# A decode kernel with two attention parts: a shorter unrolled head ahead of VectorE's loop, and a third buffer for output weights

## The chip, the cores and the metric

The kernel runs on one core of one Trainium2 chip. The metric is the device time of one execution in microseconds, lower is better. Executions of one kernel differ by some us (the kernel before: 1383.4 to 1388.7 in its first six), so each comparison below uses several executions of both kernels on one chip. The span on a profile page is some 2.1 us shorter than the time of the same execution.

## The reference

Two independent decode attentions on one token, four batches, head size 128, 512 model columns; their outputs are joined side by side.

```python
def _A_ref(x, k_cache, v_cache, wq, wo):      # "sliding" part: 32 query heads, 8 KV heads
    W = min(4096, max(256, Sk // 4))          # Sk = 8192, so W = 2048: only the last 2048 positions
    q = (x @ wq).reshape(B, Sq, Hq, Dh) ...
    k = jnp.repeat(k_cache[:, :, Sk - W:, :], rep, axis=1)      # v likewise, rep = 4
    p = softmax(einsum("bhqd,bhkd->bhqk", q, k) * Dh ** -0.5)
    return einsum("bhqk,bhkd->bhqd", p, v) ... @ wo

def _B_ref(x, k_cache, v_cache, wq, wo):      # "full" part: 32 heads, the whole cache of 8192
    ...                                       # the same without the window and the repeat
return jnp.concatenate([a, b], axis=-1)
```

Nearly all bytes are the caches: 2 x 268 MB for the full part, 2 x 16.8 MB for the sliding part.

## The kernel before

Work is cut into 72 chunks: 0 to 7 are the sliding part (2 MB of keys and 2 MB of values each), 8 to 71 the full part (4 MB and 4 MB). For every chunk TensorE transposes the key tiles into PSUM (`tr`), VectorE and ScalarE copy them to SBUF (`kt`), TensorE multiplies them with the queries (`sc`), and the softmax and the product with the values (`po`) follow one chunk later. SyncE issues all loads in a fixed order; each waits until its place in `kv`, ten halves of 2 MB, is free.

```python
NWO = 2                                    # buffers of the sliding part's output weights
...
HALF_A = {"k": (8, 9), "v": (6, 7)}        # halves of kv for sliding keys and values
...
def dma_wo(g):                             # output weights of sliding chunk g
    dst = wor[:, g % NWO, :] ...
    sch.add_dma("sp", lambda e: e.dma_start(dst, src), "d_wo%d" % (g % NWO),
                waits=[("fin", g - NWO)] if g >= NWO else [], key=("wo", g))
...
def dma_kv(kind, c):
    at = HALF_A[kind][c % 2] if ch["ab"] == 0 else (0 if kind == "k" else 4) + 2 * (c % 2)
    waits = take((kind, c), at, 1 if ch["ab"] == 0 else 2, ("T", ch["s_last"]) if kind == "k" else ("pv", c))
    ...
    sch.add_dma("sp", lambda e: e.dma_start(dst, src), "d_h%d" % at, waits=waits, key=(kind, c))
```

So full keys use halves 0 to 3, full values 4 to 7, and keys of chunk c wait for the last transpose of chunk c - 2.

Each engine's program is first recorded straight, with a mark before every second chunk. Stretches between marks that are the same but for fixed steps then become one loop; everything ahead of them stays unrolled.

```python
def emit_looped(self, engname, eng, sems, loop):
    for first, n, a, step in self.runs(engname):       # equal stretches between marks
        self.emit_ops(ops[done:m[first]], eng, sems)   # unrolled part
        with loop(0, n) as i:
            self.emit_ops(ops[m[a]:m[a + 1]], eng, sems, step, i, a - first)
...
sch.emit_looped("dve", e, sems, loop_on(mybir.EngineType.DVE, 0))   # slot 0: aligned loop head
```

At the first full chunk there is no chunk before it, so a dummy chunk (`NONE`) stands in. Its VectorE work differs from the later ones, so VectorE's stretch of chunks 8 and 9 doesn't match and stays unrolled:

```python
def norm_sum(c):
    if c == NONE:
        pe_mm(ms[:, L0:L0 + 4], onesf[:, :], rst[1][:, :], waits=ms_read, key=("L", c))
        sch.add("dve", lambda e: e.memset(rz[:, :], 0.0), waits=[("L", c)], key=("rinv", c))
        sch.add("dve", lambda e: e.memset(oz[:, :], 0.0), key=("rz", c))
        ...
        return
    ...
def norm_out(c):
    if c == NONE:
        sch.add("dve", lambda e: e.memset(oz[:, :], 0.0), waits=[("pv", c), ("rz", c)], key=("oT", c))
        ...
```

## Time and profile before

| what | value | read from |
|---|---|---|
| median, 3 runs | 1384.63 us (1383.43 to 1386.19) | times |
| profiled execution | 1388.1 us (span 1386.0) | times and page |
| bytes, mean rate | 587.56 MB, 424 GB/s | page, slices |
| steady rate, 200 to 1340 us | 431 GB/s | stretches |
| packets of the instruction queue q14 | 8 of 8 KiB | page, queues; sizes from the trace |

In the lines of profiles below, `[6.16 <-issue]` says that the engine stood idle for 6.16 us just before, and that the profile shows nothing that it waited for; `<-PE tr` names what it waited for. A load lands when its bytes are there; its 16 transfer engines finish one by one, so it has a first and a last landing (values 10 in before: 183.43 and 186.70 us). A hole is a stretch in which the load queue runs dry.

### The profile page before, as it was taken

The page shows a single profiled execution, that of the slowest core. Times are in us where ns is not written, and L with a number is a line of the kernel's source. Part 1 is how long each engine was busy: PE and PEld are TensorE (multiplying, and loading weights), DVE is VectorE, ACT ScalarE, POOL GpSimd, SP SyncE. Part 2 cuts the span into 40 slices and gives each one's busy share as a digit, 9 for nine tenths or more (in the row PEclk, how much of TensorE's full clock was granted, in tenths as well). Part 3 has the DMA queues.
Part 4 walks back from the last instruction along what each step waited for, and adds up shares of the span by engine and source line. Part 5 has one row for each costly group of instructions (what it writes and reads, how often), then busy time and mean ns, then how long its engine had stood idle before and what let it go on. Part 6 is the DMA issues. An engine that isn't in the chain of part 4 may idle for free.

```text
span 1386.0 us, 59254 instructions
## 1 busy us (share of the span) xinstructions
PE 1181.4 (85%) x26901; PEld 1137.5 (82%) x26901; DVE 640.3 (46%) x1337; ACT 436.2 (31%) x649; POOL 4.5 (0%) x16
## 2 busy tenths in 40 slices
PE   4888789888888888888898889888988889888988
PEld 4776789887888888887888888887988888787987
DVE  1665355444444444444444445444444445444443
ACT  1553233332333223332333223232332233232332
POOL 1000000000000000000000000000000000000000
PEclk9998999999999999999999999999999999999998
DMA  9999989999999999999999999999999999999997
GB/s 400 414 416 410 424 351 429 431 436 429 428 431 434 427 432 433 428 432 430 431 427 436 430 427 436 430 428 429 436 430 427 436 430 427 430 436 429 428 431 320
DMA packets 30088, 587.56 MB, mean 424 GB/s; under 512 B 2784, under 2 KB 10992, under 8 KB 11248
## 3 DMA queue, kind: packets, MB, share of 16 engines
q1 hardware_dynamic: 30040, 587.22, 99.1%
q8 instruction: 16, 0.26, 0.1%
q14 instruction: 8, 0.07, 0.0%
q10 hardware_dynamic: 24, 0.01, 0.0%
HBM read 587.21 MB, written 0.01 MB: 424 GB/s over the span
## 4 chain that ended last, share of the span: by engine, by line
DMA 59%; PE 37%; DVE 2%; issue 1%; ACT 0%; SPq 0%; ACTq 0%; DVEq 0%
DMA kv<-in_B_k_cache_dram 57%; PE tr L367 21%; PE sc L369 10%; PE po L369 3%; PE fin L369 2%; DMA kv<-in_B_wq_dram 2%; DVE sA L482 1%; PE ms L369 1%; DVE kt L431 0%; DVE rm L491 0%; DVE sA L480 0%; ACT pba L545 0%; PE ms L367 0%; DVE outsb L640 0%; ACT kt L429 0%
## 5 line engine op out<-in xcount | busy, mean ns | idle before, releaser
L367 PE MATMUL tr<-identb,kv 128*128 128x128 bf16 x8704 | 705.5, 232 | 156.6 <-DMA kv<-in_B_k_cache_dram 154.3
L431 DVE COPY kt<-tr 128x1024 bf16<-128x1024 bf16 x736 | 502.6, 691 | 478.2 <-PE tr L367 471.6
L367 PEld LDWEIGHTS tr<-identb,kv 128*128 128x128 bf16 x8704 | 560.9, 105 | 182.1 <-issue 97.6
L429 ACT ACTIVATE kt<-tr 128x1024 bf16<-128x1024 bf16 x352 | 360.2, 1024 | 635.5 <-PE tr L367 634.9
L369 PE MATMUL sc<-qb,kt 128*128 128x64 bf16 x8704 | 449.6, 197 | 15.7 <-DVE kt L431 15.4
L369 PEld LDWEIGHTS sc<-qb,kt 128*128 128x128 bf16 x8704 | 371.5, 101 | 19.8 <-DVE kt L431 17.2
L369 PE MATMUL po<-pbb,kv 128*128 128x64 bf16 (+1 forms) x8320 | 293.9, 191 | 6.6 <-issue 6.6
L369 PEld LDWEIGHTS po<-pbb,kv 128*128 128x128 bf16 x8320 | 267.0, 97 | 8.6 <-issue 6.9
L530 ACT ACTIVATE pbb<-sc,negb 64x128 bf16<-64x128 f32 x128 | 51.2, 400 | 295.9 <-DVE negb L520 295.2
L496 DVE TENSOR_REDUCE rm<-sc 64x1 f32<-64x128 f32 x128 | 37.0, 289 | 92.5 <-PE sc L369 91.6
L508 DVE TENSOR_REDUCE gm<-ms 1x2 f32<-1x128 f32 (+1 forms) x72 | 20.1, 279 | 44.5 <-PE ms L367 44.4
L520 DVE COPY negb<-ms 128x1 f32<-128x1 f32 (+1 forms) x72 | 11.4, 159 | 57.4 <-PE ms L369 57.4
L369 PE MATMUL ms<-identf,gx 1*128 1x1 f32 (+1 forms) x144 | 27.7, 259 | 0.0
L369 PEld LDWEIGHTS ms<-identf,gx 1*128 1x128 f32 (+1 forms) x144 | 21.5, 187 | 4.9 <-issue 0.9
L530 ACT ACTIVATION_READ_ACCUMULATOR pbb<-sc,negb 64x1 f32 x128 | 23.7, 185 | 0.0
L367 PE MATMUL ms<-identf,rm 128*1 128x128 f32 (+1 forms) x72 | 19.6, 273 | 2.3 <-DVE rm L491 2.3
L369 PE MATMUL po<-pba,kv 128*128 128x64 bf16 x512 | 20.1, 199 | 0.5 <-ACT pba L545 0.5
L369 PE MATMUL fin<-wos,oz 128*4 128x512 bf16 x66 | 20.0, 385 | 0.3 <-DVE oz L620 0.3
L369 PEld LDWEIGHTS po<-pba,kv 128*128 128x128 bf16 x512 | 17.9, 102 | 0.6 <-ACT pba L545 0.6
L512 DVE TENSOR_SCALAR gx<-gm 1x128 f32<-1x128 f32 (+1 forms) x72 | 15.9, 221 | 2.5
L369 PE MATMUL ms<-xT,kv 128*128 128x4 bf16 x256 | 7.1, 166 | 8.6 <-DMA kv<-in_A_wq_dram 4.4
L369 PEld LDWEIGHTS ms<-xT,kv 128*128 128x128 bf16 x256 | 7.0, 104 | 8.8 <-DMA kv<-in_A_wq_dram 4.5
(49 smaller groups left out, 138.3 us busy)
## 6 DMA issues: line engine op xcount, KB each, us to landing
kv<-in_B_k_cache_dram SPq DMA_DIRECT2D x64, 4096.0 KB, 26.5
kv<-in_B_v_cache_dram SPq DMA_DIRECT2D x63, 4096.0 KB, 31.4
kv<-in_A_k_cache_dram SPq DMA_DIRECT2D x8, 2048.0 KB, 13.7
kv<-in_A_v_cache_dram SPq DMA_DIRECT2D x8, 2048.0 KB, 15.8
kv<-in_A_wq_dram SPq DMA_DIRECT2D x1, 4096.0 KB, 12.4
kv<-in_B_wq_dram SPq DMA_DIRECT2D x1, 4096.0 KB, 27.5
wor<-in_A_wo_dram SPq DMA_DIRECT2D x8, 512.0 KB, 10.7
wos<-in_B_wo_dram SPq DMA_DIRECT2D x16, 256.0 KB, 22.0
```

Of the source, the lines that this page charges most:

```text
L367: sch.add("pe", lambda e: e.transpose(o, l, r), waits, key)
L369: sch.add("pe", lambda e: e.matmul(o, l, r, start=start, stop=stop), waits, key)
L429: sch.add("act", lambda e: e.activation(dst, src, ACTF.Copy), waits=waits, key=("ev", s))
L431: sch.add("dve", lambda e: e.tensor_copy(dst, src), waits=waits, key=("ev", s))
L482: emit = lambda e, src=src, b=b: e.scalar_tensor_tensor(out=t, in0=src, scalar=mk[:, b:b + 1], in1=t, op0=ALU.mult, op1=ALU.add)
L496: sch.add("dve", lambda e, src=src, pp=pp: e.tensor_reduce(out=rm[pp, m, 0:1], in_=src, axis=AX.X, op=ALU.max), waits=[("S", ch["s_last"]) ...
L508: sch.add("dve", lambda e: e.tensor_reduce(out=gm[0:C, m, 0:U], in_=src, axis=AX.X, op=ALU.max), waits=[("trm", c)], key=("gmax", c))
L512: sch.add("dve", lambda e: e.tensor_scalar(out=dst, in0=gv, scalar1=-scale, scalar2=None, op0=ALU.mult), waits=[("gmax", c)], key=("gx", c))
L520: sch.add("dve", lambda e: e.tensor_copy(negb[:, m, 0:C], ms[:, col:col + C]), waits=[("bc", c)], key=("negb", c))
L530: sch.add("act", lambda e, src=src, pp=pp, n=n, u=u: e.activation(pbv[pp, :, u], src, ACTF.Exp, bias=negb[pp, m, 0:1], scale=scale, accum_ ...
```

## The change

Intent: "VectorE and ScalarE enter their loops with the tensor engine, the absent chunk masked by zeros; last sliding-block output weights have a buffer of their own". The dummy chunk gets the same VectorE instructions as every later chunk: its reciprocal runs on ones, its mask is a block of zeros in front of `pm`. So VectorE's stretch of chunks 8 and 9 matches and joins the loop. The weights of sliding chunk 7 get a third buffer, which moves the sliding values and one weight load to other halves of `kv`.

```diff
-NWO = 2
+NWO = 3
...
-        pm = sb("pm", [P, HB // 2, 2, 2, 4], F32)
+        pm = sb("pm", [P, HB // 2 + 1, 2, 2, 4], F32)
...
+            sch.add("pool", lambda e, own=own: e.memset(own, 1.0), ...)      # cut: ones for the dummy sums
...
-        HALF_A = {"k": (8, 9), "v": (6, 7)}
+        HALF_A = {"k": (8, 9), "v": (4, 5)}
...
+        def wo_slot(g):
+            return g % 2 if g < NCA - 1 else 2
...
-            sch.add_dma("sp", lambda e: e.dma_start(dst, src), "d_wo%d" % (g % NWO),
-                        waits=[("fin", g - NWO)] if g >= NWO else [], key=("wo", g))
+            sch.add_dma("sp", lambda e: e.dma_start(dst, src), "d_wo%d" % slot,
+                        waits=[("fin", g - 2)] if g >= 2 and slot < 2 else [], key=("wo", g))
...
-        dma_wq(1, 2)
+        dma_wq(1, 6)
...
         def norm_sum(c):
-            if c == NONE:
-                ... three memsets and a return, as shown above
+            if c >= NCA or c == NONE:
+                pair = 4 * (c - NCA - 1 + 4) if c != NONE else 8             # masks start with zeros
...
         def norm_out(c):
-            if c == NONE:
-                sch.add("dve", lambda e: e.memset(oz[:, :], 0.0), ...)
```

More of the change, by code (lines that the diff above doesn't have):

```diff
@@ L262, in bass_concat_heads__sliding_block_cached__mha_block_cached__decode_kernel @@
             fill=0.0, base=0, channel_multiplier=-1), waits=["c_onesf"], key="c_identf")
-        sch.add("pool", lambda e: e.memset(rst[1][:, :], 0.0), key="c_rs")
-        sch.add("pool", lambda e: e.memset(qb[:, :, :], 0.0), key="c_qb")
+        sch.add("pool", lambda e: e.memset(rst[1][:, :], 0.0), key="c_rs0")
+        for u in range(2):
+            own = rst[1][u * P // 2:(u + 1) * P // 2, :].rearrange("p (b u) -> p u b", u=2)[:, u, :]
+            sch.add("pool", lambda e, own=own: e.memset(own, 1.0), waits=["c_rs0"], key="c_rs" if u else None)
+        sch.add("pool", lambda e: e.memset(qb[:, :, :], 0.0), waits=["c_rs"], key="c_qb")
         sch.add("pool", lambda e: e.memset(pm[:, :, :, :, :], 0.0), key="c_pm0")
         for x in range(2):
-            sch.add("pool", lambda e, x=x: e.memset(pm[:, :, x, x, :], 1.0), waits=["c_pm0"], key="c_pm" if x else None)
+            sch.add("pool", lambda e, x=x: e.memset(pm[:, 1:, x, x, :], 1.0), waits=["c_pm0"], key="c_pm" if x else None)
         sch.add("pool", lambda e: e.memset(pbt[0][:, :, :], 0.0), key=("c_pb", 0))
@@ L295, in dma_wq @@
             sch.add_dma("sp", lambda e: e.dma_start(flat(at, 2), src), "d_h%d" % at, waits=waits, key=("wq", ab))
+        def wo_slot(g):
+            return g % 2 if g < NCA - 1 else 2
         def dma_wo(g):
             src = A_wo[g * 4 * P:(g + 1) * 4 * P, :].rearrange("(hl d) n -> d hl n", d=P)
-            dst = wor[:, g % NWO, :].rearrange("p (hl n) -> p hl n", hl=4)
-            sch.add_dma("sp", lambda e: e.dma_start(dst, src), "d_wo%d" % (g % NWO),
-                        waits=[("fin", g - NWO)] if g >= NWO else [], key=("wo", g))
+            slot = wo_slot(g)
+            dst = wor[:, slot, :].rearrange("p (hl n) -> p hl n", hl=4)
+            sch.add_dma("sp", lambda e: e.dma_start(dst, src), "d_wo%d" % slot,
+                        waits=[("fin", g - 2)] if g >= 2 and slot < 2 else [], key=("wo", g))
         def dma_wos(hp):
@@ L583, in norm_sum @@
         def norm_sum(c):
-            if c == NONE:
-                pe_mm(ms[:, L0:L0 + 4], onesf[:, :], rst[1][:, :], waits=ms_read, key=("L", c))
-                sch.add("dve", lambda e: e.memset(rz[:, :], 0.0), waits=[("L", c)], key=("rinv", c))
-                sch.add("dve", lambda e: e.memset(oz[:, :], 0.0), key=("rz", c))
-                ms_read[:] = [("rinv", c)]
-                rs_read[NSM] = [("L", c)]
-                return
-            if chunks[c]["ab"] == 0:
+            if 0 <= c < NCA:
                 m, n, rs, ri = c % NSM, 16, rst[0][:, c % NSM, :], rinv[:, c % NSM, :]
@@ L594, in norm_sum @@
                 m, n, rs, ri = NSM, 4, rst[1][:, :], rinv[:, 0, 0:4]
-            pe_mm(ms[:, L0:L0 + n], onesf[:, :], rs, waits=[("rs", c), "c_onesf"] + ms_read, key=("L", c))
+            pe_mm(ms[:, L0:L0 + n], onesf[:, :], rs, waits=([("rs", c), "c_onesf"] if c != NONE else []) + ms_read, key=("L", c))
             sch.add("dve", lambda e: e.reciprocal(out=ri, in_=ms[:, L0:L0 + n]), waits=[("L", c)], key=("rinv", c))
-            if chunks[c]["ab"] == 1:
-                pair = 4 * (c - NCA - 1)
+            if c >= NCA or c == NONE:
+                pair = 4 * (c - NCA - 1 + 4) if c != NONE else 8
                 pv = pm[:, :, :, :, :].rearrange("p a b c d -> p (a b c d)")
@@ L607, in norm_out @@
         def norm_out(c):
-            if c == NONE:
-                sch.add("dve", lambda e: e.memset(oz[:, :], 0.0), waits=[("pv", c), ("rz", c)], key=("oT", c))
-                po_read[:] = [("oT", c)]
-                return
-            if chunks[c]["ab"] == 0:
+            if 0 <= c < NCA:
                 m = c % NSM
@@ L618, in norm_out @@
                 i1 = rz[:, :].rearrange("p (x y) -> p x y", x=2)
-            waits = [("rinv" if c < NCA else "rz", c), ("pv", c)] + ([("fin", c - 2 if c != NCA + 1 else NONE)] if c >= 2 else [])
+            waits = [("rinv" if 0 <= c < NCA else "rz", c), ("pv", c)] + ([("fin", c - 2 if c != NCA + 1 else NONE)] if c >= 2 else [])
             sch.add("dve", lambda e: e.tensor_tensor(out=o, in0=i0, in1=i1, op=ALU.mult), waits=waits, key=("oT", c))
@@ L630, in emit_fin @@
             else:
-                w = wor[:, c % NWO, :].rearrange("p (hl n) -> p hl n", hl=4)
+                w = wor[:, wo_slot(c), :].rearrange("p (hl n) -> p hl n", hl=4)
                 ov = oT[:, c % NSM, :].rearrange("p (u c) -> p u c", c=REP)
```

## The prediction

> **What bounds the kernel now.** The page comes first. It says that bytes bound this kernel: 587 MB pass, the transfer engines are in use in nearly every slice, and the chain that ended last is mostly the load of the full cache's keys.
>
> ```profile
> DMA  9999989999999999999999999999999999999997
> GB/s 400 414 416 410 424 351 429 431 436 429 428 431 434 427 432 433 428 432 430 431 427 436 430 427 436 430 428 429 436 430 427 436 430 427 430 436 429 428 431 320
> ...
> DMA 59%; PE 37%; DVE 2%; issue 1%; ACT 0%; SPq 0%; ACTq 0%; DVEq 0%
> ```
>
> The reader is to see the rate of about 430 that holds from slice 7 to 39, and one hole in it: slice 6, 173 to 208 us, with 351. As the bytes stay the same, only the holes can be won. A table by stretch sizes them (columns: stretch, length, busy time of each engine, granted clock, DMA share, GB/s).
>
> ```profile
> 103.00:113.00 10.00, 8.30 (x120) 6.44 (x117) 6.61 (x18) 5.19 (x8) 0.00 (x0) 0.83 0.91 359
> ...
> 130.00:183.00 53.00, 41.51 (x861) 40.06 (x859) 20.70 (x42) 14.11 (x20) 0.00 (x0) 0.87 1.00 425
> 183.00:190.00 7.00, 7.00 (x178) 7.00 (x177) 4.48 (x9) 3.07 (x3) 0.00 (x0) 1.00 0.19 70
> 190.00:200.00 10.00, 10.00 (x258) 9.86 (x255) 5.57 (x13) 3.49 (x7) 0.00 (x0) 1.00 0.99 406
> 200.00:1340.00 1140.00, 988.62 (x22818) 961.51 (x22816) 530.96 (x1084) 353.15 (x529) 0.00 (x0) 0.94 1.00 431
> ```
>
> Against its neighbours' 425 GB/s, the hole at 183 us cost 7 x (1 - 70/425) = 5.8 us, the refill after it 10 x (1 - 406/431) = 0.6 us, and a small hole at 103 to 113 us 10 x (1 - 359/425) = 1.6 us. Together 8.0 us of 1385, that is 0.6%. From 200 to 1340 us nothing is to be had.
>
> Why the queue ran dry is read from the issues on SyncE's queue. Chunks 0 to 7 are the sliding part, 8 to 71 the full part; a full chunk has a key and a value load of 4 MB, at 4.19 MB / 430 GB/s = 9.75 us each.
>
> ```profile
> 103.25 0.54 SPq L322 DMA_DIRECT2D kv<-in_A_v_cache_dram  x1
> 111.05 0.37 SPq L300 DMA_DIRECT2D wor<-in_A_wo_dram  x1
> ...
> 161.41 0.33 SPq L334 DMA_DIRECT2D kv<-in_B_k_cache_dram  x1
> 170.40 0.33 SPq L334 DMA_DIRECT2D kv<-in_B_v_cache_dram  x1
> 189.00 0.33 SPq L334 DMA_DIRECT2D kv<-in_B_k_cache_dram  x1
> ```
>
> The load of 170.40 (values 10) has landed on the first engine at 183.4 us, on the last at 186.7 (the trace's semaphore events). The next, keys 12, waits until TensorE has transposed chunk 10 and goes out at 189.00. TensorE was late because VectorE stood still:
>
> ```profile
> 169.94 0.16 DVE L443 COPY qb<-qs 128x2 bf16<-128x2 bf16 x1
> 176.26 1.29 DVE L431 COPY kt<-tr 128x1024 bf16<-128x1024 bf16 x2 [6.16 <-issue]
> ```
>
> ```profile
> 168.52 0.80 PE L369 MATMUL po<-pbb,kv 128*128 128x64 bf16 x22 [3.45 <-issue]
> ...
> 177.01 0.61 PE L369 MATMUL sc<-qb,kt 128*128 128x64 bf16 x8 [4.16 <-DVE kt L431]
> ```
>
> The 6.16 us sit between the branch into VectorE's loop and its first instruction, with no semaphore to wait for. [...] ScalarE enters its loop too, at 130 us, and there branch and first instruction are 0.5 us apart.
>
> [...] a packet of the instruction queue starts at 174.2 us, inside the 6.16 us. [...] the packets of VectorE's and ScalarE's queue are of 8192 bytes (TensorE's of 16384)[...]. [...] the trace shows 0.50 from 176.5 to 182.6 us, behind the 4.16 us stop.
>
> **The change part by part.**
>
> 1. VectorE's loop. The built programs differ by 37 VectorE instructions: chunks 8 and 9 leave the unrolled part (192 instructions become 155) and the loop runs 31 times in place of 30. ScalarE's program is the same, in spite of the description: it runs 32 times already. Where does the branch land? Single instruction packets start at 58.0 and 152.7 us, when VectorE has done 50 and 178 recorded instructions. The difference is 128[...]. So the 6.16 us should not move to 129 us but vanish, down to ScalarE's 0.5 us.
>
> What that gives: chunk 10's keys part starts at 170.18 us in both. The next chunk, undisturbed, needs 204.85 - 193.78 = 11.1 us for it. The fetch stall of TensorE's own first pass (3.45 us at 165 to 168.5) stays, and with it the half clock of 169.6 to 172.7 us, worth some 1.3 us. Keys 12 are issued at 170.2 + 11.1 + 1.3 = 182.6, in place of 189.00.
>
> 2. The buffer for the last output weights. Now the weights of 111.05 us wait for a free buffer, and behind them the full part's first loads. With a third buffer they go out at about 104 us. At that time 7.7 us of work is pending (values 7 lands first at 111.0), and weights and keys 8 and 9 add 9.2 MB = 21.3 us, so the queue lasts to 132.3 us and the hole of 1.6 us closes. In the trace values 8 landed first at 144.4; they would land at 142.1, 2.3 us earlier.
>
> 3. Moved halves of the buffer. Sliding values now sit where values 8 go, so that load waits for the last sliding product, 127.4 us, in place of going out at 113.0. The queue lasts to 132, so nothing is lost. Values 9 wait for the absent chunk's product at 148 us as before.
>
> 4. Masks. Two memsets of 64x2 on GpSimd, done near 5 us, in a stretch where it has nothing else of use, and a reciprocal and two products (0.18 + 0.17 + 0.17 us by the later rows) for three memsets of 0.06 on VectorE, which has 0.67 us gaps there. Zero.
>
> The sum, by first landings: values 8 at 142.1, keys 10 at 151.8, values 9 at 161.6. Keys 11 are issued at 161.4 as before, since TensorE's first pass (128.87 to 170.18 us for what later takes 31) is held by its own fetches. A new load needs 0.95 us to its first packet (189.00 to 189.95), so 0.8 us are lost; keys 11 land at 172.1, values 10 at 181.9. Keys 12, issued at 182.6, start at 183.6: 1.7 us lost. They land at 193.3, against 200.7 before: 7.4 us. But the last engine counts. It lagged by 3.3 us ahead of the hole and by 0.5 us after it, as the hole let it catch up; the two short gaps let it catch up by only 2.5, so 0.8 remain: last landing 194.1 against 201.16, 7 us at best. Restarts and uneven engines will take some of it; I put the gain at 5.5 us. From there all is bound by bytes, and the gain is carried to the end: 1384.6 - 5.5 = 1379.1 us.
>
> **The rivals.**
> (a) The stall moves with the branch: [...] VectorE fetches at 130 us. Then keys 8 end some 5 us late, keys 10 go out at 145 while the queue is dry at 142, and everything TensorE does until 180 us shifts. Against it: ScalarE's entry at the same time took 0.5 us[...]. It would leave 1 to 3 us of gain: 1382 to 1384.
> (b) TensorE's own fetches are what bounds 128 to 183 us, so that the early gain of part 2 is taken back at keys 11 and 12. For it: four stops "issue" of 0.7 to 3.5 us in that pass. It is partly in my sum; in full it leaves about 4 us: 1380.5.
> (c) The stall is fully hidden by the byte bound. Against it: the 70 GB/s. It would give 1384.6.
> (d) Both holes close without new ones: 8.0 us, 1376.6.
>
> **Range and chances.** The runs before spread over 1383.4 to 1386.2, so a median is good to about 1 us. Low is (d) less that, 1376.0; high is (a), 1383.0. 2% would be 27.7 us, over three times all holes together, so faster gets 0.01; slower by as much would need a new wait in every round of a loop whose instructions are the same, 0.01.
>
> **What would show it.** The idle "issue" row of VectorE's copies into kt gone (6.2 us to under 1); keys 12 issued near 182.6 us; the output weights issued behind values 7 at 104; a stretch 183 to 190 us at over 330 GB/s and 103 to 113 at 420; 431 GB/s from 200 to 1340 as before. I am wrong if VectorE stops for 6 us at 130, or if keys 12 come at 187 or later, or if a new hole over 3 us opens between 140 and 185.

Cut from the recorded text, at the marks, is what it told of the hardware that no trace or run of this case shows; the expectations below have cuts of the same kind. With it goes the reason why the stop was to vanish rather than move: a count of where VectorE's branch and its loop head lie. No term of the sum is cut. The sum assumes that the stop is gone, and comes to keys 12 issued at 170.2 + 11.1 + 1.3 = 182.6 us and landed last at 194.1 in place of 201.16, 7 us at best, put at 5.5: 1384.6 - 5.5 = 1379.1 us. The 0.50 is the granted TensorE clock.

## More of the kernel before

From the profile page of the kernel before: the busy times of the engines, then two rows of the DMA queues (packets, MB, share of 16 engines' span).

```profile
PE 1181.4 (85%) x26901; PEld 1137.5 (82%) x26901; DVE 640.3 (46%) x1337; ACT 436.2 (31%) x649; POOL 4.5 (0%) x16
...
q1 hardware_dynamic: 30040, 587.22, 99.1%
...
q14 instruction: 8, 0.07, 0.0%
```

The reader is to see that the load queue takes 99.1% of all engines' time while TensorE is at 85%: this kernel is bound by bytes, and less than 1% of the span has transfer engines without a load.

## The result, and the profile after

| | before | after |
|---|---|---|
| median of 6 runs | 1385.76 us (1383.43 to 1388.65) | 1381.39 us (1380.30 to 1381.74) |
| ratio, 95% interval | | 0.9967 (0.9954 to 0.9980) |
| span of the profiled execution | 1386.0 | 1379.5 |

Ratios are the mean time of one kernel's runs over that of the other's of the same rounds, so not quite the ratio of the medians quoted. The gain is 4.4 us by medians and 4.6 by the ratio (0.0033 x 1385.8), 0.3%. The two spans differ by 6.5 us, but the profiled execution of before was a slow one, 1388.1 us, 2.4 above the median of six.

The page of the kernel after: span, slices, chain and instruction queue.

```profile
span 1379.5 us, 59295 instructions
...
GB/s 401 414 417 424 427 410 431 431 430 430 431 429 435 427 433 430 430 432 429 434 427 434 431 429 431 430 432 429 434 429 431 431 430 432 429 434 429 431 431 319
...
q14 instruction: 6, 0.05, 0.0%
```

Slice 6 rose from 351 to 410 GB/s, all slices after it stand where they stood, and two instruction packets are gone. The stretches of the kernel after (columns as in the prediction; the last three are granted TensorE clock, DMA share and GB/s):

```profile
103.00:113.00 10.00, 8.29 (x168) 7.11 (x166) 6.65 (x18) 6.10 (x9) 0.00 (x0) 1.00 1.03 408
130.00:183.00 53.00, 44.66 (x992) 43.39 (x990) 23.27 (x46) 15.92 (x22) 0.00 (x0) 0.90 1.00 423
183.00:190.00 7.00, 7.00 (x183) 6.86 (x180) 4.19 (x11) 2.06 (x6) 0.00 (x0) 1.00 0.96 360
190.00:200.00 10.00, 10.00 (x256) 9.51 (x253) 5.38 (x9) 3.96 (x4) 0.00 (x0) 1.00 1.01 436
200.00:1340.00 1140.00, 984.52 (x22690) 957.24 (x22687) 529.34 (x1081) 351.32 (x527) 0.00 (x0) 0.93 1.00 431
```

The hole at 183 us went from 70 to 360 GB/s and the small one at 103 from 359 to 408; the steady 1140 us are untouched. VectorE around its loop entry in the kernel after:

```profile
126.03 0.68 DVE L638 CAST outsb<-fin 4x512 bf16<-4x512 f32 x1 [1.26 <-PE fin L377]
126.77 1.29 DVE L439 COPY kt<-tr 128x1024 bf16<-128x1024 bf16 x2
```

The first copy inside the loop follows the last unrolled instruction by 126.77 - 126.71 = 0.06 us. Before, the first loop copy came 6.16 us late. The stop did not move, it is gone. SyncE's issues after:

```profile
103.62 0.60 SPq L308 DMA_DIRECT2D wor<-in_A_wo_dram  x1
...
104.81 0.94 SPq L342 DMA_DIRECT2D kv<-in_B_k_cache_dram  x2
124.52 0.33 SPq L342 DMA_DIRECT2D kv<-in_B_v_cache_dram  x1
...
159.72 0.33 SPq L342 DMA_DIRECT2D kv<-in_B_k_cache_dram  x1
...
181.44 0.33 SPq L342 DMA_DIRECT2D kv<-in_B_k_cache_dram  x1
```

The output weights go out at 103.62 us where they waited until 111.05, and keys 12 at 181.44 in place of 189.00.

### The profile page after: what moved, and what is told of

It reads as the page before. It is cut to its first block, busy times and chain, and to the rows that moved or that the text cites. A ratio compares the mean times of both kernels' runs of the same rounds, so it can differ in the third digit from the quotient of the medians.

```text
span 1379.5 us, 59295 instructions
## 1 busy us (share of the span) xinstructions
PE 1175.3 (85%) x26901; PEld 1132.3 (82%) x26901; DVE 640.6 (46%) x1337; ACT 435.7 (32%) x649; POOL 4.8 (0%) x18
## 4 chain that ended last, share of the span: by engine, by line
DMA 59%; PE 37%; DVE 2%; issue 1%; ACT 0%; SPq 0%; ACTq 0%; DVEq 0%
DMA kv<-in_B_k_cache_dram 57%; PE tr L375 22%; PE sc L377 10%; PE po L377 3%; DMA kv<-in_B_wq_dram 2%; PE fin L377 2%; DVE sA L490 1%; PE ms L377 1%; DVE kt L439 0%; DVE rm L499 0%; DVE sA L488 0%; ACT pba L553 0%; PE ms L375 0%; ACT kt L437 0%; DVE sA L546 0%
## 5 line engine op out<-in xcount | busy, mean ns | idle before, releaser
L377 PE MATMUL sc<-qb,kt 128*128 128x64 bf16 x8704 | 448.0, 196 | 11.1 <-DVE kt L439 10.7
```

The costliest lines, as they stand in the source:

```text
L377: sch.add("pe", lambda e: e.matmul(o, l, r, start=start, stop=stop), waits, key)
```

## The experiments

Twelve runs were made, in four batches, each batch sharing its runs of the kernel before. Where a trace is quoted it is of one execution. The interval of a ratio is about 0.2% wide to each side, 2.6 us, so differences below that are not resolved by a single comparison.

| run | edit | median us | ratio to before (95%) |
|---|---|---|---|
| after_again | the change itself | 1381.34 | 0.9969 (0.9951 to 0.9988) |
| loop_only | change without its buffer part | 1381.12 | 0.9972 (0.9954 to 0.9991) |
| buffer_only | before with the buffer part | 1384.49 | 1.0002 (0.9981 to 1.0023) |
| head_free | before, loop head of VectorE not aligned | 1382.12 | 0.9973 (0.9955 to 0.9992) |
| head_free_buffer | the same and the buffer part | 1381.20 | 0.9968 (0.9948 to 0.9987) |
| pad_16 | change, 16 more VectorE instructions | 1380.80 | 0.9964 (0.9944 to 0.9983) |
| pad_32 | change, 32 more | 1381.35 | 0.9965 (0.9947 to 0.9984) |
| pad_48 | change, 48 more | 1385.71 | 1.0002 (0.9982 to 1.0021) |
| split_keys | change, all full key loads halved | 1383.67 | 0.9984 (0.9965 to 1.0003) |
| split_last | change, last key load alone halved | 1378.52 | 0.9960 (0.9940 to 0.9979) |
| split_two | change, key loads 12 and 71 halved | 1380.22 | 0.9964 (0.9946 to 0.9982) |
| split_last_again | split_last once more | 1378.55 | 0.9958 (0.9940 to 0.9977) |

The theory to be tested, as far as runs can decide it: VectorE's stop of 6.16 us, inside which a packet of the instruction queue starts (174.18 us), belongs to the entry branch into the aligned loop and depends on how many instructions stand ahead of it; the stop delayed chunk 10's transposes, so keys 12 were issued late and the load queue ran dry. The change cuts the unrolled part from 192 to 155 instructions, and with that the stop. Rivals: the gain comes from the buffer; or it comes from the masked instructions themselves; or from the early loop entry as such, however many instructions stand ahead of it.

### The change again, and its two parts one by one

> The changed kernel once more, as the yardstick for the runs beside it. Every theory expects a ratio to the kernel before near the first one, 0.9967 (0.995 to 0.998), VectorE's idle 'issue' ahead of its copies into kt under 1 us, and keys 12 issued near 181.5 us.

It repeated: 0.9969, keys 12 issued at 178.29 us. (The issue time moves by some us between executions; see the end of this part.)

```diff
  loop_only, against the kernel after:
-NWO = 3
+NWO = 2
-        HALF_A = {"k": (8, 9), "v": (4, 5)}
+        HALF_A = {"k": (8, 9), "v": (6, 7)}
-            return g % 2 if g < NCA - 1 else 2
+            return g % 2
-        dma_wq(1, 6)
+        dma_wq(1, 2)
```

> The masks and VectorE's earlier loop alone; two weight buffers and the old places of the halves, as in the kernel before. My theory: VectorE's 6.2 us stop is gone, keys 12 come near 182 us, and as the queue with the small hole left at 103 to 113 us holds work until 183.4, no hole opens at 183. So this part alone gives the whole gain: ratio 0.9967, within 0.0008 of the changed kernel. Rival, the parts add up: the hole of 1.6 us at 103 to 113 stays as a loss, ratio near 0.998.

The stretch at the hole in loop_only:

```profile
183.00:190.00 7.00, 7.00 (x156) 6.51 (x154) 4.11 (x6) 3.26 (x4) 0.00 (x0) 1.00 1.01 435
```

435 GB/s: no hole at all, keys 12 issued at 176.28 (182 was expected), no stop on VectorE, and 0.9972: the loop part alone gives as much as the whole change, within the intervals.

```diff
  buffer_only, against the kernel before (the mirror of it):
-NWO = 2
+NWO = 3
-        HALF_A = {"k": (8, 9), "v": (6, 7)}
+        HALF_A = {"k": (8, 9), "v": (4, 5)}
+        def wo_slot(g):
+            return g % 2 if g < NCA - 1 else 2
...                                            # cut: dma_wo and its reader take wo_slot, as in the change
-        dma_wq(1, 2)
+        dma_wq(1, 6)
```

> The third weight buffer and the moved halves alone; VectorE enters its loop at chunk 10 as before. My theory: the output weights go out at 104 us and the hole at 103 to 113 closes, but keys 12 still come near 188 to 189 us behind the 6.2 us stop, so that the hole at 181 to 190 grows by the same 1.6 to 2.3 us: ratio 0.999 to 1.000. Rival, the parts add up: ratio near 0.9988.

First the hole's stretch, then VectorE's first copy in the loop, both of buffer_only:

```profile
183.00:190.00 7.00, 7.00 (x206) 6.94 (x202) 3.14 (x7) 1.93 (x2) 0.00 (x0) 1.00 0.62 225
```

```profile
173.08 1.29 DVE L434 COPY kt<-tr 128x1024 bf16<-128x1024 bf16 x2 [5.33 <-issue]
```

The weights and the first full keys went out early as intended (keys 8 at 104.03 us), yet the stop of 5.33 us is still there, keys 12 come at 185.60, and the hole with them. They were expected at 188 to 189; this execution began chunk 8 at 125.2 us, 3.6 earlier than the traced one of before, and all behind it is earlier by as much. Ratio 1.0002; up to 2.6 us of gain would be inside its interval, but none shows. So the two parts don't add: each of them alone or together works on the same budget, the bytes that can be delivered by the time keys 12 are issued. Bytes brought in earlier only make the queue run dry earlier, as long as the issue of keys 12 stands.

One caution for reading the traces of this stretch: chunk 8 started its keys part at 125.9 us in the profiled execution of after and at 127.6 in after_again, the same kernel; at 128.9 in before and 130 in head_free and pad_32. Such shifts move all issue times behind them. So the times above were judged with the durations of stops, which don't depend on it.

### Is it the entry into the aligned loop?

```diff
  head_free, against the kernel before:
-            sch.emit_looped("dve", e, sems, loop_on(mybir.EngineType.DVE, 0))
+            sch.emit_looped("dve", e, sems, loop_on(mybir.EngineType.DVE))
```

The work and its order stay. VectorE's loop head is no longer aligned, and with that the branch that enters the loop goes: the trace has 30 branches of this loop in place of 31, the first only at 201.48 us, behind the first round.

> The kernel before, with one word changed: VectorE's loop head is not aligned[...]. Chunks 8 and 9 stay unrolled, no masks, two weight buffers. [...] the stop at 170 us is gone (under 1 us), keys 12 near 182 to 183 us, ratio 0.996 to 0.9975, as with the masks. Rival, the stop belongs to entering the loop two chunks late, or to any entry into a loop: the stop stays at about 6 us and the ratio at 1.000.

VectorE's first loop copy in head_free:

```profile
170.75 1.29 DVE L431 COPY kt<-tr 128x1024 bf16<-128x1024 bf16 x2 [0.55 <-PE tr L367]
```

The 6.16 us that ended with "issue" are 0.55 us that end with TensorE's product, keys 12 go out at 180.76, and the ratio is 0.9973. This one option gives as much as the whole change, within the intervals, with no mask, no longer loop and no third buffer. This rules out that the masked instructions or the early entry as such are needed. It shows that the stop hangs on the entry branch, but not on what else: the branch itself is gone. For that there are the kernels that keep it, after and loop_only above and the three that follow.

> The kernel before with the third weight buffer and moved halves and the unaligned loop head on VectorE, no masks. My theory: the same as the changed kernel, ratio 0.9965 within 0.0008, keys 12 near 181.5 us. Rival, the masks matter in themselves: slower than the changed kernel by over 0.1%.

With the buffer part on top (the two diffs above together) the ratio was 0.9968, keys 12 at 179.84. As expected, the change's gain is had without its main edit.

The other direction is to bring the stop back with the change in place, by idle instructions on VectorE ahead of the loop:

```diff
  pad_16, pad_32, pad_48 (N = 16, 32, 48), against the kernel after:
+        pads = sb("pads", [P, N], F32)
...
+        for i in range(N):
+            sch.add("dve", lambda e, i=i: e.memset(pads[:, i:i + 1], 0.0))
```

They run at the very start, where VectorE has little else to do (busy 0.55 of the first 10 us in before).

> The changed kernel with 16 memsets of one column on VectorE at its very start, where it waits for data anyway. [...] no stop near 127 us (under 1 us), ratio as the changed kernel (0.996 to 0.998). [...]

> As the run with 16, but 32 memsets: [...] My theory: VectorE stops for 4 to 7 us at its loop entry near 127 us with no semaphore to wait for, TensorE waits behind it, keys 10 are issued 3 to 6 us later than with 16, and the ratio is 0.998 to 1.000 (gain of 0 to 3 us left). Rival[...]: no stop and the same time as with 16, within 0.1%.

> The changed kernel with 48 memsets in front of VectorE's program. The run with 32 did not stop at its loop entry, [...] the block ahead of the loop has 155 + 32 = 187 instructions there and 192 in the kernel before, which stops; the edge lies between. With 48 it has 203 and is past it. [...] a stop 'issue' of 4 to 7 us on VectorE at its loop entry near 127 to 130 us, keys 10 issued at 141 to 146 us (136 to 141 in the other runs), and a ratio of 0.998 to 1.000. Rival, [...] no stop, 0.9967.

VectorE's first loop copy in pad_32, then in pad_48, then the stretch in which pad_48 loses:

```profile
130.76 1.29 DVE L442 COPY kt<-tr 128x1024 bf16<-128x1024 bf16 x2
```

```profile
134.17 1.29 DVE L442 COPY kt<-tr 128x1024 bf16<-128x1024 bf16 x2 [5.81 <-issue]
```

```profile
130.00:183.00 53.00, 43.19 (x948) 42.06 (x949) 23.79 (x48) 15.15 (x22) 0.00 (x0) 0.90 0.92 390
```

With 16 and with 32 more instructions there is no stop (ratios 0.9964 and 0.9965). With 32 a stop of 4 to 7 us was expected: a miss. With 48 the stop is back, 5.81 us, now at the loop entry near 130 us. Keys 10 go out at 146.95 in place of 136.97, the queue is dry until 147.93, and the stretch falls from 423 to 390 GB/s, 53 x (1 - 390/423) = 4.1 us. The ratio is 1.0002: the whole gain is lost, by 16 instructions that cost nothing themselves. The instruction queue tells the same: 8 packets in before, buffer_only and pad_48, the three kernels with the stop that were looked at, and 6 in after, loop_only, head_free, head_free_buffer, pad_16 and pad_32.

The times of these packets, which the trace has, say more. In the three kernels that stop, a packet starts ahead of VectorE's branch (152.69 us in before, 150.62 in buffer_only, 109.99 in pad_48, with 178 to 180 of VectorE's recorded instructions done); in after, loop_only, pad_16 and pad_32 there is none. And the stop has the same two parts each time: 3.3 to 4.2 us from the branch to its packet, then 2.1 us to the first copy (in before 170.02, 174.18 and 176.26).

This sets the edge. Unrolled parts of 155 + 32 = 187 instructions pass, 192 (before) and 155 + 48 = 203 don't. The seven kernels named that have an aligned head all fit an edge between 187 and 192; why it lies there is not shown.

### Can the rest of the hole be had?

In the profiled after, 183 to 190 us still stood at 360 GB/s, and the last chunk's work follows the last byte. If key loads are issued in two halves of 2 MB, the first half can start when half of chunk c - 2 is transposed.

```diff
  split_keys, against the kernel after:
+            if kind == "k" and ch["ab"] == 1:
+                mid = ch["s"] + ch["NG"] // 2 - 1
+                for h in range(2):
+                    waits = take((kind, c), at + h, 1, ("T", ch["s_last"] if h else mid))
+                    sch.add_dma("sp", lambda e, h=h: e.dma_start(kv[:, at + h, :], src[:, h * 8192:(h + 1) * 8192]),
+                                "d_h%d" % (at + h), waits=waits, key=("k2", c) if h else (kind, c))
...                                            # cut: TensorE waits for ("k2", c) at half of the chunk
```

> The changed kernel with each key load of the full part in two halves of 2 MB with a semaphore each: the first half of a buffer is given free when TensorE has transposed half of the chunk. My theory: what is left of the hole at 183 us is that keys 12 wait for the end of chunk 10's transposes; the first half goes out near 176 us, the stretch 183 to 190 rises from 360 to about 425 GB/s (1.1 us), and at the end the last chunk's transposes start earlier, worth about 0.6 us as the last values then bound it: 1 to 2 us under the changed kernel, ratio 0.9953 to 0.996. Rival, TensorE's own fetch stops bound that stretch whatever the loads do, or twice as many loads cost as much as they give: no change, 0.9967.

```profile
183.00:190.00 7.00, 7.00 (x159) 6.87 (x156) 4.49 (x9) 3.59 (x7) 0.00 (x0) 1.00 0.98 419
...
200.00:1340.00 1140.00, 987.80 (x22734) 956.31 (x22732) 528.96 (x1083) 352.97 (x528) 0.00 (x0) 0.94 1.01 429
```

The stretch stands at 419 GB/s in split_keys. But with whole loads it stands at 412 to 445 in the eight other traces without the stop (412 in after_again, the same kernel as after), so the 360 belonged to one execution, and that the split closed a hole is not shown. The median was 1383.67, 2.3 us over after_again's 1381.34 and over pad_32's 1381.35 of the same batch: a miss. The steady rate fell: 430.9 to 429.3 GB/s between 300 and 1300 us, where all other traces have 430.8 to 431.1. Over the 1140 us of the stretch that is an estimated 1140 x 1.6/431 = 4.2 us, more than the hole was worth. Which part of the edit costs it was not tested apart. A packet of the key loads is 16 KiB in place of 32; two took 2 x 0.616 = 1.232 us where one took 1.218, and the packets of 4 bytes, 16 to a load in after, rose from 1840 to 2650 between 300 and 1300 us. So halve only where it helps: at the end.

```diff
  split_last (SPLIT = (71,)) and split_two (SPLIT = (12, 71)), against the kernel after:
+            if kind == "k" and c in SPLIT:
+                for h in range(2):
+                    x = slice(h * 8192, (h + 1) * 8192)
+                    w = [("T", chunks[c - 2]["s"] + chunks[c - 2]["NG"] // 2 - 1)] if h == 0 else waits
+                    sch.add_dma("sp", lambda e, x=x: e.dma_start(dst[:, x], src[:, x]), "d_h%d" % (at + h),
+                                waits=w, key=("k2", c) if h else (kind, c))
+                return
...
+            if kind == "k":      # other loads: SyncE raises the second semaphore itself, so the loop stays uniform
+                sch.add("sp", lambda e: e.sem_inc(sems[name], 16), self_inc=True)
...
+                    waits += [("k2", c)] if ("k2", c) in sch.tk and g == chunks[c]["NG"] // 2 else []
```

> The changed kernel with the key load of the last chunk alone in two halves (for all others SyncE just raises the second half's semaphore, so that TensorE's loop stays uniform). Splitting all keys cost more than it gave, as a 16 KiB packet takes 0.616 us against 1.218 for 32 KiB, 430.9 to 429.3 GB/s. Theory: this one split costs under 0.1 us and lets the last transposes start 4.9 us earlier, so that the end is bound by the last values: from their last landing to the end about 4.3 us (6.4 in most runs): 1 to 2 us under the changed kernel, ratio 0.9953 to 0.996. Rival, the tail is bound otherwise: 0.9967.

> The kernel with the last keys in two halves once more, as its interval (0.994 to 0.9979) overlaps that of the changed kernel (0.9951 to 0.9988). If it is faster: median near 1378.5 us again, below the changed kernel's 1381.3, last landing to end about 4.4 us in the profile; if the first run was luck: 1381.

TensorE's end in the kernel after, then in split_last:

```profile
1372.29 3.42 PE L377 MATMUL po<-pbb,kv 128*128 128x2 bf16 x128
1376.04 1.01 PE L377 MATMUL fin<-wos,oz 128*4 128x512 bf16 x2 [0.33 <-DVE oz L618]
```

```profile
1368.17 3.19 PE L389 MATMUL po<-pbb,kv 128*128 128x2 bf16 x112
1372.00 0.59 PE L389 MATMUL po<-pbb,kv 128*128 128x2 bf16 x16 [0.64 <-DMA kv<-in_B_v_cache_dram]
```

In after all 128 last products run in one piece, with no data waited for: TensorE is late, as it still had to transpose the last keys. In split_last it has done 112 of them before the last bytes come, waits 0.64 us for data and has 16 left. From the last landing to the end of the span it took 4.5 us (1371.96 to 1376.42), as in split_last_again and split_two, against 4.9 in after and 6.3 to 7.5 in the nine other traces with whole key loads. The landing itself is not outstanding: it was at 1371.8 in loop_only and at 1374.7 in after. So the gain is read from the tail. The medians are 1378.52 and 1378.55 on two chips, some 6 us under the kernel before in the same rounds (1384.93 and 1384.56). The changed kernel did not run in these batches: its medians of 1381.39 and 1381.34 are 2.8 us higher, but by the ratios to before (0.9967 and 0.9969 against 0.9960 and 0.9958) it is 1 to 1.5 us, and the intervals overlap. Of split_last's 11 executions 9 took at most 1379.1 us, of the changed kernel's 12 only one. So it is faster, by an estimated 1 to 3 us.

> As before, with the keys of chunk 12 in halves too, the first of them released at half of chunk 10. Theory: what is left of the hole at 183 us is under 1 us in most runs, so 0 to 0.8 us under the run with the last keys split; rival: nothing, or slower by the extra wait of the queue.

With keys 12 halved too the stretch at 183 us stands at 419 GB/s, where split_last and its repeat, with whole keys 12, have 435 and 431; and it brought no further time: 1380.22, ratio 0.9964 against 0.9960, inside each other's interval. What the rest of the hole is worth stays unresolved; in the execution of after that showed it, it is at most about 1 us (7 x (1 - 360/425) = 1.1).

## Why the prediction was right, and where a term was off

The time on record was 1379.1 us with a range of 1376.0 to 1383.0; measured 1381.4. The chain from the stop to the hole held, the gain was 4.4 us in place of 5.5. The other 1.1 us of the miss are the starting point: it reckoned from 1384.6, the median of three runs, and six have 1385.8. The step from its sum, "7 us at best", to 5.5 had no working ("restarts and uneven engines will take some of it"); that the time came this near is in part luck.

- **VectorE's stop vanishes rather than moves**: right. 0.06 us at the entry after; head_free shows that it hangs on the entry branch, pad_48 that with this branch in place 16 instructions more ahead of it bring it back. The count under it is cut from the record, and pad_32, for which it had expected a stop, shows that it was off. The error fell on the safe side: 32 instructions more than after has still pass.
- **Keys 12 at 182.6**: right, 181.44 in the profiled execution; first landing 193.84 against 193.3 predicted.
- **The lag, "so 0.8 remain: last landing 194.1"**: this is the mis-sized term. The two short gaps were to let the last engine catch up by 2.5 us; it caught up by 1.2 (3.57 behind at keys 11, 2.42 at keys 12) and landed keys 12 at 196.26. Between the traces, the first landing moved by 200.69 - 193.84 = 6.85 us but the last by 201.16 - 196.26 = 4.90, and the last landing of keys 71 by 1360.06 - 1355.11 = 4.95. The old hole had let the slowest transfer engine catch up (lag 3.27 before it, 0.47 after it), so part of the hole was not lost time for the engine that sets the end: by the landings it stood idle from 186.70 to 189.95, 3.25 us. By the other 1.8 of the 4.90 it was ahead already at values 10 (184.90 against 186.70), which includes the shift from one execution to another. The 4.9 us of this pair of traces go with the 4.4 to 4.6 that the times show. Later the lag is 1.6 to 2.0 us from keys 13 to the end of before; in after it grows, while the queue never runs dry, from 2.42 to 3.13 and then to 3.84 us, both times at the loads that landed just behind an instruction packet (462.7 and 1349.1 us).
- **The buffer, "they would land at 142.1, 2.3 us earlier"**: the mechanism was right (weights at 103.62, values 8 landing first at 142.46) but it adds nothing to the hole at 183. The prediction's own sum has that, though it does not say so: the landing of keys 12 follows from their issue at 182.6, and the 2.3 us are lost again as its "0.8" and "1.7". Only its total of all holes, 8.0 us, and rival (d) count both. buffer_only brought nothing that shows, and loop_only the whole gain.
- **The moved halves** cost nothing, as said: values 8 go out at 124.52, before the queue's end at an estimated 132.
- **Masks, zero**: VectorE is busy 640.6 us against 640.3.
- **Rival (a)**, the stall moves to 130 us: did not happen, but pad_48 made it happen. It leaves no gain, rather than the 1 to 3 us given. **Rival (b)**, TensorE's own fetches take the gain back: in part. Its stops are still there after (7.3 us in the value products of the first pass): four stops "issue" of 1.5, 2.5, 1.0 and 3.4 us, where before has 0.7, 2.4, 0.7 and 3.5, each ending 2.3 to 2.6 us behind the start of a 16 KiB packet of the instruction queue q8. And the stretch at 183 us is at 360 and not 425, but after_again, the same kernel, has 412 there and loop_only 435, so this varies between executions. **(c)**, fully hidden, is refuted by 0.9967; **(d)**, 8.0 us, by the same.

A small misreading: the half clock (0.50) behind the stops is read as 169.6 to 172.7 and 176.5 to 182.6 us; the trace's clock record has 169.2 to 172.6 and 176.1 to 182.9.

The description's ScalarE half is empty: ScalarE's program is the same in both kernels, with 32 rounds already before.

## What to carry to other kernels

In a kernel bound by bytes, look for the stretch in which the load queue runs dry, follow back which issue was late, and fix only that. Here it was one branch, with an instruction packet inside its stop of 6.16 us, and one alignment option of VectorE's loop did as much (0.9973) as a rewrite of the dummy chunk; a stop "issue" of 5 to 6 us right at a loop entry is the sign to look for. Size such a hole by the slowest transfer engine's idle time rather than by the mean rate, don't add gains that share one budget, and look last at what follows the final byte, where halving a single load gave another 1 to 3 us.
